# Attention and two expert layers on one core: zero rows copied by ScalarE, zeros behind the running sum, three warming products, changed times in the planner

## The chip, the core and the metric

One Trainium2 chip, one of its cores. The time is that of one execution on the device in microseconds; a kernel is run several times and the median counts. Five engines work side by side, each through its own queue in order: TensorE (PE, with weight loads PEld), VectorE (DVE), ScalarE (ACT), GpSimd (POOL) and SyncE (SP), which here issues every DMA.

## What is computed

```python
scores = scale * np.matmul(q, k.transpose(0, 1, 3, 2))      # 4 batches, 8 heads, 576 x 64
log_f = np.log(np.clip(f, 0.0001, 1.0))
cum = np.cumsum(log_f, axis=-1)
scores = np.where(causal, -1e9, scores + cum[..., None] - cum[..., None, :])
attn = softmax(scores)                                       # by row
x = (attn @ v), heads side by side                           # 2304 tokens x 512
x = ((x @ w1) * (x @ w2)) @ w3 @ w_out                       # 512 -> 1024 -> 512
xn = x / sqrt(mean(x * x) + 1e-6) * rms_g
out = (silu(xn @ w_gate) * (xn @ w_val)) @ w_out2            # 512 -> 1536 -> 512
```

## The kernel before

**The work.** Up to about 400 us the kernel does three things at once. (1) Attention, 32 heads one after another. A head's scores are products of Q and K with extra rows that add the running sum of log f (L421 for heads 0 and 1, which use `rq` and `rk` in plain float32; L423 and L424 later, which use Q and K split into a high and a low part). VectorE takes the row maximum (L443) and ScalarE the exponential (L451); TensorE transposes the result (L492), ScalarE copies the high part (L501, `PTh`), VectorE takes the difference, the low part (L502 and L505, `PTl`), and TensorE multiplies by V into `wide` (L552, L556). The two buffers a and b serve even and odd heads. (2) Weights come as 64-bit numbers and are made into float32 by `convert`: the load (L575), the high halves on ScalarE (L584), the low halves on ScalarE (L588) or VectorE (L590), both joined on VectorE (L594). A `unit` then splits the result into two parts for TensorE (L258, L260, L251). `widen` makes three sums more (L819), which the second layer needs, and stores the matrix to `sw_d` (L842); ten of these are done beside attention, in one buffer `raw_w`. (3) The first layer: w3 x w_out is multiplied out ahead (L668), then come, by blocks of 464 tokens, x @ w1 and x @ w2 (L705), their product (L712, L713) and the rest (L730). From about 530 us on the second layer runs on TensorE alone (L920, L1001).

**The start** (`start`, from L1092). `f` is loaded in two halves and clipped (L1113, VectorE); ScalarE takes the logarithm (L1114) and VectorE the running sum `cum` of each half (L1119); from it VectorE makes Q's extra rows of heads 0 and 1 (L1133) and ScalarE K's (L1136). These rows lie in the lower 64 partitions of `rq` and `rk`, which must be zero elsewhere: `make_rows` writes zeros, for head 0 on VectorE and for head 1 on GpSimd (L1099, L1100). `make_zeros` (L348) writes the corners of the buffers of scores, which no product fills. Five products of zeros (L1090, WARM) run on TensorE before the first head; three and one more come a little later (`zeros` in `attention`).

**What sets the order.** No engine's order is written out by hand. Every step is handed to `Plan` with the engines that could do it, a duration in ns for each, the keys it reads and writes, and for some a due time (S0, TE, T1 for heads, WD0 and WD1 for the ten stores of widened matrices, FD and FR for the first layer). `Plan.order` then lays the steps out in time by these numbers, on the engine that would end a step first, and what it finds is the order in which the instructions are written to the queues. DMA0, COLD, RS and RB are its numbers for DMAs and for the first products. A key that a step reads only for the plan (`zeros` reads CUM) makes no wait on the chip unless the data itself is read.

## Time and profile before

| | us |
|---|---|
| median of 3 runs (931.03 to 933.44) | 931.06 |
| the profiled execution | 929.87 |
| its span, first to last instruction | 928.2 |
| busy: TensorE / VectorE / ScalarE / GpSimd | 913.6 / 803.3 / 550.0 / 165.0 |

The profile is of one execution. A busy TensorE includes products that overlap, so its share is no measure of how full it is; its idle time, and the chain of work that ended last, say more. In a row of a timeline the first number is the start in us from the beginning of the span, the second how long the work lasted, then engine, line, operation, what is written from what, and in brackets how long the engine had been idle and what ended that. Line numbers are those of the kernel before; in the changed one those of `start` are two to five higher, those from L349 to L505 one, and those from L575 to L1090 four.

### The profile page before, as it was taken

How to read it: one execution, taken by the hardware profiler on the slowest of the kernel's cores; microseconds unless marked ns; L12 is line 12 of the kernel's file. 1: busy time of each engine (PE TensorE's matmuls, PEld its weight loads, DVE VectorE, ACT ScalarE, POOL GpSimd, SP SyncE). 2: the span in 40 equal slices, each digit the busy share in tenths (PEclk: the TensorE clock that was granted, in tenths of full speed). 3: DMA queues.
4: the chain of work that ended last, by engine and by line, in shares of the span. 5: the costliest groups of instructions: out<-in, count | busy, mean ns of one | idle time of the engine just before them, and what ended most of it. 6: DMA issues, size and time to landing. Idle time of an engine off the chain costs nothing.

```text
span 928.2 us, 14651 instructions
## 1 busy us (share of the span) xinstructions
PE 913.6 (98%) x5064; PEld 845.6 (91%) x5064; DVE 803.3 (87%) x1540; ACT 550.0 (59%) x1132; POOL 165.0 (18%) x162
## 2 busy tenths in 40 slices
PE   9999999999999999999999999999999999999998
PEld 5678888899989898988899999999999999999998
DVE  7999999988999899836655889999988899888796
ACT  8999888777777776732332344545444465544452
POOL 2254423343223422230120400000000000000000
PEclk9999999999999999999999999999999999999999
DMA  7867476667755584437777334634743425633322
GB/s 258 298 226 235 136 274 217 232 184 239 264 175 181 155 285 175 153 109 282 237 269 259 121 131 133 217 103 130 258 168 119 143 69 171 203 119 122 134 68 103
DMA packets 50878, 170.70 MB, mean 184 GB/s; under 512 B 7388, under 2 KB 23356, under 8 KB 43636
## 3 DMA queue, kind: packets, MB, share of 16 engines
q1 hardware_dynamic: 50804, 169.77, 54.8%
q8 instruction: 40, 0.66, 0.3%
q14 instruction: 34, 0.28, 0.1%
HBM read 133.28 MB, written 32.63 MB: 179 GB/s over the span
## 4 chain that ended last, share of the span: by engine, by line
PE 82%; DVE 9%; DMA 5%; ACT 2%; issue 2%; SPq 0%; DVEq 0%; ACTq 0%
PE bank L920 28%; PE bank L705 17%; PE bank L730 10%; PE bank L1001 8%; PE wide L1001 4%; PE bank L492 3%; PE wide L552 3%; PE bank L668 3%; DVE qk L251 1%; DMA raw_w<-in_w 1%; PE bank L423 1%; PE bank L424 1%; DVE wbig L251 1%; DVE PTl L502 1%; PE bank L1090 1%
## 5 line engine op out<-in xcount | busy, mean ns | idle before, releaser
L705 PE MATMUL bank<-xhl,wbig 128*128 128x464 f32 (+1 forms) x960 | 216.6, 374 | 1.1 <-DVE wbig L251 1.1
L705 PEld LDWEIGHTS bank<-xhl,wbig 128*128 128x128 f32 x960 | 176.2, 188 | 18.6 <-DVE wbig L251 1.5
L920 PE MATMUL bank<-xop,wbig 128*128 128x384 f32 x1008 | 182.3, 334 | 0.7 <-ACT cs L944 0.7
L920 PEld LDWEIGHTS bank<-xop,wbig 128*128 128x128 f32 x1008 | 175.5, 188 | 1.1 <-ACT cs L944 1.0
L920 PE MATMUL bank<-xop,lbig 128*128 128x384 f32 x504 | 94.7, 334 | 0.0
L920 PEld LDWEIGHTS bank<-xop,lbig 128*128 128x128 f32 x504 | 88.0, 188 | 0.0
L502 DVE TENSOR_TENSOR PTl<-bank,PTh 128x512 fp32r<-128x512 f32 (+5 forms) x138 | 62.8, 469 | 7.9 <-ACT PTh L501 7.1
L501 ACT CAST PTh<-bank 128x320 fp32r<-128x320 f32 (+4 forms) x138 | 57.5, 435 | 18.3 <-PE bank L492 15.2
L730 PE MATMUL bank<-uh,Wch 128*128 128x464 f32 (+1 forms) x160 | 60.7, 379 | 0.0
L730 PE MATMUL bank<-uh,Wcl 128*128 128x464 f32 (+1 forms) x160 | 59.4, 371 | 0.0
L730 PE MATMUL bank<-ul,Wch 128*128 128x464 f32 (+1 forms) x160 | 59.3, 371 | 0.0
L251 DVE TENSOR_TENSOR lbig<-zf,lbig 128x768 fp32r<-128x768 f32 x63 | 59.2, 952 | 0.1
L1001 PE MATMUL bank<-lbig,wbig 128*128 128x384 f32 x324 | 57.9, 334 | 0.0
L1001 PEld LDWEIGHTS bank<-lbig,wbig 128*128 128x128 f32 x324 | 56.3, 188 | 0.0
L258 ACT ACTIVATE lbig<-zf 128x768 fp32r<-128x768 f32 x39 | 33.0, 849 | 37.6 <-PE bank L1001 17.9
L260 POOL TENSOR_SCALAR lbig<-zf 128x768 fp32r<-128x768 f32 x2 | 1.8, 920 | 276.7 <-DVE zf L819 263.5
L552 PE MATMUL wide<-PTh,V 128*128 128x512 f32 (+4 forms) x145 | 44.4, 316 | 1.4 <-DVE nmaxb L443 0.6
L712 DVE TENSOR_TENSOR u<-bank,u 128x464 f32<-128x464 f32 (+1 forms) x40 | 25.2, 629 | 23.1 <-PE bank L705 22.9
L251 DVE TENSOR_TENSOR wbig<-nrm,wbig 128x768 fp32r<-128x768 f32 (+1 forms) x42 | 43.3, 1036 | 0.4
L713 ACT CAST uh<-u 128x464 fp32r<-128x464 f32 (+1 forms) x40 | 23.0, 575 | 34.4 <-DVE u L712 34.4
L942 ACT COPY cs<-bank 128x384 f32<-128x384 f32 x36 | 17.3, 481 | 42.8 <-PE bank L920 42.8
L926 DVE TENSOR_TENSOR zf<-cs 128x384 f32<-128x384 f32 x72 | 39.9, 554 | 2.7 <-ACT cs L931 1.7
(271 smaller groups left out, 2109.5 us busy)
## 6 DMA issues: line engine op xcount, KB each, us to landing
xf<-sw_d SPq DMA_DIRECT2D x24, 896.0 KB
wbig<-w_d SPq DMA_DIRECT2D x12, 1024.0 KB
nrm<-sw_d SPq DMA_DIRECT2D x12, 896.0 KB
raw_w<-in_wgv SPq DMA_DIRECT2D x10, 1024.0 KB
sw_d<-raw_w SPq DMA_DIRECT2D x10, 896.0 KB
rk<-in_k SPq DMA_DIRECT2D x62, 144.0 KB
nrm<-wo_d SPq DMA_DIRECT2D x11, 768.0 KB
xf<-wo_d SPq DMA_DIRECT2D x10, 768.0 KB
```

Of the source, the lines that this page charges most:

```text
L251: plan.op([t_dve(n, lock=True), t_pool(n)], lambda e: on[e].tensor_sub(*(x() if callable(x) else x for x in (o, a, b_))), r, w)
L258: A.activation(o_, a_, AF.Copy, scale=by)
L492: T.transpose(o[:, c * P:(c + 1) * P], PB[p][i][:, kb * P:(kb + 1) * P], ident)
L501: act(n, lambda c=c, to=to, n=n: A.copy(PTh[:, to:to + n], o[:, c:c + n]), [], [("PTh", name), key], at, 55)
L502: dve(m, lambda c=c, to=to, m=m: V.tensor_sub(PTl[:, to:to + m], o[:, c:c + m], f32(PTh[:, to:to + m])), [("PTh", name)], [("PTl", name), ...
L552: pe(w, lambda s_=s_, o=o, w=w, c=c, kb=kb, m=m, src=src: T.matmul(t[:, o:o + w], V2[p][:, kb, :], src[:, c:c + w], start=(s_ == 0 and m = ...
L668: T.matmul(o, a, b_, start=(ft == 0 and m == 0), stop=(ft == KF - 1 and m == 2))
L705: T.matmul(o, a, x[:, kt, :], start=(kt == 0 and i == 0), stop=(kt == KD - 1 and i == 2))
L730: T.matmul(o, a[:, es], x[:, ft, 0:w], start=(q == 0 and ft % 2 == 0 and i == 0), stop=(q == 3 and ft % 2 == 1 and i == 2))
L920: T.matmul(o, w[:, a, POS[j], kt], x[c][:, kt], start=start and kt == 0 and i == 0, stop=kt == 1 and i == 2, skip_group_check=not start)
L926: plan.op([t_dve(TH, lock=True), t_pool(TH)], lambda e: on[e].tensor_mul(o(), x(), y()), r, w)
L1001: T.matmul(tiles[m], wv[:, a, k, m], z[c][:, kt], start=start and k == 0 and x == 0, stop=k == KH - 1 and x == 2, skip_group_check=not start)
```

## The change

ScalarE copies the zero rows of head 1 from head 0's, which VectorE writes in two steps; GpSimd writes them no more. `make_zeros` begins with a multiplication that reads the first half of `cum`, so that the zeros really wait for the first scan. WARM goes from 5 to 3. The rest are numbers of the planner: due times (S0, T1, WD1, FD), its start of DMAs, and durations of six kinds of step. They change no instruction, but the engine that takes a step where there is a choice, and the order on every engine.

```diff
--- before.py
+++ after.py
@@ -40,12 +40,12 @@
 SW = 2 * NOP * 256
 PADW = 8
 EARLY = 10
-WD0, WD1 = 130000, 380000
+WD0, WD1 = 130000, 400000
 WD2, WD3 = 420000, 520000
 NR = 4
 KH = KF2 // 2
 FROWS = 112
-WARM = 5
+WARM = 3
 NQ, NP, QD, PAIR = 2, 3, 6, 10
 WIDER = 3
 NST = 3
@@ -53,16 +53,16 @@
 
 
 
-S0, TE, T1 = -1500, 7800, 13400
+S0, TE, T1 = -2500, 7800, 13800
 LT, LP = 5000, 13000
 
 WC0, WCP = 20000, 9000
 
-FD, FR = 27000, 1.8
+FD, FR = 25000, 1.8
 
 WAIT, SLIP, SLIP0, SOON = 5.0, 1200, 300, 30000
 
-DMA0, COLD, RS, RB = 2500, 7000, 230, 330
+DMA0, COLD, RS, RB = 550, 6000, 230, 330
 MT, MARGIN, MARGIN2 = 135000, 600, 700
 MT2, MARGIN3 = 538000, 200
 
@@ -346,6 +346,7 @@
         G.memset(one32, 1.0)
 
     def make_zeros():
+        G.tensor_scalar(out=PB[0][1][0:1, QEND[1]:QEND[1] + 1], in0=cum[0:1, 0:1], scalar1=1.0, scalar2=1.0, op0=ALU.mult, op1=ALU.mult)
         for t in PB:
             for i in range(1, 4):
                 G.memset(t[i][:, QEND[i]:], 0.0)
@@ -502,7 +503,7 @@
             dve(m, lambda c=c, to=to, m=m: V.tensor_sub(PTl[:, to:to + m], o[:, c:c + m], f32(PTh[:, to:to + m])), [("PTh", name)], [("PTl", name), key], at)
         if m < n:
             both = PTh[D:P, m:n]
-            dve(n - m, lambda: V.tensor_sub(both, o[D:P, lo + m:lo + n], f32(both)), [], [("PTh", pt), key], at)
+            dve(n - m + 110, lambda: V.tensor_sub(both, o[D:P, lo + m:lo + n], f32(both)), [], [("PTh", pt), key], at)
 
     def sums(h, at):
         pr, r_o = h // 2 % 2, r_d[h // 2].rearrange("j (i b n) -> b (j i) n", i=5, b=4)
@@ -557,8 +558,8 @@
             [("PTh", PT_KB3), ("V2", p), ("V2h", p)], wk, at)
         x_to, x_key = X[b % 2][j * D:(j + 1) * D, pp, :], ["cq"] * (b == 0) + [("x", b % 2, pp, j)] + [("raw", "x1")] * (b == 1)
         low = xlow[j * D:(j + 1) * D, :]
-        act(S, lambda: A.copy(x_to, t[0:D, 0:S]), wk, x_key, at)
-        act(S, lambda: A.copy(low, t[D:P, 0:S]), wk, [("xlow", j)], at)
+        act(S, lambda: A.copy(x_to, t[0:D, 0:S]), wk, x_key, at, 160)
+        act(S, lambda: A.copy(low, t[D:P, 0:S]), wk, [("xlow", j)], at, 160)
 
     def normalize(h, at):
         pair, (b, pp) = h // 2, divmod(h // 2, H // 2)
@@ -570,9 +571,12 @@
             dve(S, lambda: V.tensor_add(x[D:], x[D:], low[D:]), [("xlow", 1)], keys[1:])
         plan.op([t_dve(S, lock=True), t_pool(S)], lambda e: on[e].tensor_mul(x, x, rall), [("rall", 0), ("rall", 1)], keys)
 
+    begun = []
+
     def convert(raw, key, src, at_load, r_load=(), w_load=(), to=None):
         kl, kh = key + ("lo",), key + ("hi",)
-        dma(1.05e6, lambda: SP.dma_start(out=u32(raw()), in_=src.bitcast(U32)), r_load,
+        begun.append(key)
+        dma(1.36e6 if len(begun) == 1 else 1.05e6, lambda: SP.dma_start(out=u32(raw()), in_=src.bitcast(U32)), r_load,
             [key, kl, kh] + list(w_load) + ["cn", "cn1"] * (key[1] == "x1"), at_load)
 
         def lo():
@@ -589,7 +593,7 @@
             else:
                 V.tensor_scalar(out=lo(), in0=lo(), scalar1=2.0**-29, scalar2=7.0, op0=ALU.mult, op1=ALU.min)
 
-        plan.op([t_act(1024), t_dve(1024, 0.52, True)], bits, [key, "under"], [kl])
+        plan.op([t_act(1024, 260), t_dve(1024, 0.61, True)], bits, [key, "under"], [kl])
         o, w = (lo, [kl]) if to is None else (lambda: u32(to()), [kl, kh])
         dve(1024, lambda: V.scalar_tensor_tensor(out=o(), in0=hi(), scalar=3, in1=lo(), op0=ALU.logical_shift_left, op1=ALU.bitwise_or), [key, kh], w, lock=True)
         return lo, hi
@@ -1095,29 +1099,27 @@
         load_qk(0, -90)
         dma(2e3, load_g, w=["g"], at=50000)
         dve(300, lambda: V.memset(mask, 0.0), w=["mask", "mask0"])
-        def make_rows(e, p):
-            e.memset(rq[p][D:P, :], 0.0)
-            e.memset(rk[p][D:P, :], 0.0)
-
-        dve(1030, lambda: make_rows(V, 0), w=[("nrowq", 0), ("nrown", 0), ("rk", 0, 1)])
+        for x, keys in ((rq, [("nrowq",)]), (rk, [("nrown",), ("rk", 1)])):
+            w0, w1 = ([(k[0], p, *k[1:]) for k in keys] for p in range(2))
+            dve(515, lambda x=x: V.memset(x[0][D:P, :], 0.0), w=w0)
+            act(S, lambda x=x: A.copy(x[1][D:P, :], x[0][D:P, :]), w0, w1)
 
         for i in range(WARM):
             zeros(5, -1000)
         pool(580, make_ones, w=["one32", "cn1"], at=-50)
         pool(1100, make_masks, w=["ident", "mask", "ones"], at=-40)
-        pool(1160, lambda: make_rows(G, 1), w=[("nrowq", 1), ("nrown", 1), ("rk", 1, 1)])
         dve(70, lambda: V.memset(rows_c, 1.0), w=["picks"])
         dve(70, lambda: (V.memset(under, -0.501), V.memset(exp_in, 0.0)), w=["under", "exp"])
         act(1500, lambda: A.activation(rows_c[:, 0:1], rows_c[:, 0:1], AF.Ln), [], ["picks"])
         for i, c in enumerate(half):
-            dve(150, lambda c=c: V.tensor_scalar(out=fc[:, c], in0=fc[:, c], scalar1=1.0e-4, scalar2=1.0, op0=ALU.max, op1=ALU.min), [], [("fc", i)], lock=True)
+            dve(170, lambda c=c: V.tensor_scalar(out=fc[:, c], in0=fc[:, c], scalar1=1.0e-4, scalar2=1.0, op0=ALU.max, op1=ALU.min), [], [("fc", i)], lock=True)
             act(S // 2, lambda c=c: A.activation(fc[:, c], fc[:, c], AF.Ln), [], [("fc", i)], fixed=200)
         for i, c in enumerate(half):
             if i:
                 x, last = fc[:, c.start:c.start + 1], cum[:, c.start - 1:c.start]
                 dve(30, lambda: V.tensor_add(x, x, last), [CUM[0]], [("fc", 1)])
             dve(S + 60, lambda c=c: V.tensor_tensor_scan(out=cum[:, c], data0=one32[:, c], data1=fc[:, c], initial=0.0, op0=ALU.mult, op1=ALU.add), [("fc", i), "one32"], [CUM[i]])
-        pool(650, make_zeros, [CUM[1]], ["zeros"])
+        pool(850, make_zeros, [CUM[0]], ["zeros"])
         hi, lo = cqx[:, 0, :], cqx[:, 1, :]
 
         def first_rows(h):
@@ -1134,7 +1136,7 @@
                 [*CUM, "ident", "picks"], [("nrowq", h)])
             for i, n in enumerate(half):
                 act(S // 2, lambda n=n: A.activation(rk[h][r, n], cum[r, n], AF.Identity, scale=c[:, 1:2], bias=e[0]),
-                    [CUM[i], "ident", "picks", ("nrown", h), ("rk", h, 1)], [("nrown", h, i)], fixed=260)
+                    [CUM[i], "ident", "picks", ("nrown", h), ("rk", h, 1)], [("nrown", h, i)], fixed=380)
 
         for h in range(NQ):
             first_rows(h)
```

Three places of the new order follow. GpSimd, the start; `tmp` holds f, ones and `cum`, `PB` and `rsum` are buffers of scores and row sums, `qk` is the split Q and K. Before:

```order
L1099 MEMSET rq_103 64x576
L1100 MEMSET rk_105 64x576
L351 MEMSET PB1a 128x64
L351 MEMSET PB2a 128x64
L351 MEMSET PB3a 128x64
L351 MEMSET PB1b 128x64
L351 MEMSET PB2b 128x64
L351 MEMSET PB3b 128x64
L353 MEMSET rsuma 128x32
L353 MEMSET rsumb 128x32
L354 MEMSET roots 128x32
L372 MEMSET qk_108 64x576
```

and with the change:

```order
L349 TENSOR_SCALAR PB1a<-tmp 1x1
L352 MEMSET PB1a 128x64
L352 MEMSET PB2a 128x64
L352 MEMSET PB3a 128x64
L352 MEMSET PB1b 128x64
L352 MEMSET PB2b 128x64
L352 MEMSET PB3b 128x64
L354 MEMSET rsuma 128x32
L354 MEMSET rsumb 128x32
L355 MEMSET roots 128x32
L373 MEMSET qk_108 64x576
```

The two writes of zero rows are gone, and the nine writes of `make_zeros` stand behind a step that reads `cum`.

ScalarE, around the conversion of the seventh widened matrix (`raw_w`, its high halves); PB3a to PB0a are the exponentials of head 26, `PTh` copies of transposed scores. Before:

```order
L560 COPY x_133<-wide 64x576
L561 COPY xlow<-wide 64x576
L584 ACTIVATE raw_w_1233<-raw_w_1233 128x1024
L451 ACTIVATE PB3a,rsumb<-PB3a,nmaxa 128x448
L501 CAST PTh<-bank_61 128x320
L451 ACTIVATE PB2a,rsumb<-PB2a,nmaxa 128x320
L451 ACTIVATE PB1a,rsumb<-PB1a,nmaxa 128x192
L501 CAST PTh<-bank_59 128x448
L501 CAST PTh<-bank_60 128x256
L258 ACTIVATE qk_108<-rq_103 64x576
L258 ACTIVATE PB1a<-PB2a 64x64
L451 ACTIVATE PB4a,rsumb<-PB4a,nmaxa 128x576
```

and with the change:

```order
L452 ACTIVATE PB3a,rsumb<-PB3a,nmaxa 128x448
L502 CAST PTh<-bank_61 128x320
L452 ACTIVATE PB2a,rsumb<-PB2a,nmaxa 128x320
L258 ACTIVATE qk_108<-rq_103 64x576
L452 ACTIVATE PB1a,rsumb<-PB1a,nmaxa 128x192
L452 ACTIVATE PB4a,rsumb<-PB4a,nmaxa 128x576
L502 CAST PTh<-bank_59 128x448
L502 CAST PTh<-bank_60 128x256
L452 ACTIVATE PB4a,rsumb<-PB0a,nmaxa 64x64
L739 COPY nrm<-bank_63 128x464
L258 ACTIVATE PB4a<-PB4a 128x64
L588 ACTIVATE raw_w_1239<-raw_w_1239 128x1024
```

The conversion stood ahead of all exponentials of head 26 and now stands behind them.

VectorE, around the three sums of the ninth widened matrix (L819 before, L823 now), with the low parts `PTl` of head 28 before, and of the head then in work now. Before:

```order
L594 SCALAR_TENSOR_TENSOR raw_w_1233<-raw_w_1233 128x1024
L502 TENSOR_TENSOR PTl<-bank_59,PTh 128x448
L502 TENSOR_TENSOR PTl<-bank_60,PTh 128x256
L819 TENSOR_TENSOR raw_w_1233<-raw_w_1233 128x512
L819 TENSOR_TENSOR raw_w_1233<-raw_w_1233 128x256 x2
L502 TENSOR_TENSOR PTl<-bank_59,PTh 128x64
L712 TENSOR_TENSOR u_134<-bank_62,u_134 128x464
```

and with the change:

```order
L598 SCALAR_TENSOR_TENSOR raw_w_1239<-raw_w_1239 128x1024
L503 TENSOR_TENSOR PTl<-bank_61,PTh 128x512
L503 TENSOR_TENSOR PTl<-bank_59,PTh 128x64
L444 ISA PB2b,nmaxb<-bank_60,mask 128x320
L444 ISA nmaxb 128x1
L444 ISA PB1b,nmaxb<-bank_60,mask 128x192
L444 ISA nmaxb 128x1
L823 TENSOR_TENSOR raw_w_1239<-raw_w_1239 128x512
L716 TENSOR_TENSOR u_134<-bank_63,u_134 128x464
L823 TENSOR_TENSOR raw_w_1239<-raw_w_1239 128x256 x2
```

The sums stood ahead of the `PTl` of 64 columns and now stand behind it and behind the next head's `PTl` of 512.

## Rows read from the trace of the kernel before

**Rows 1.** The page: span, TensorE's busy time, the chain that ended last.

```profile
span 928.2 us, 14651 instructions
...
PE 913.6 (98%) x5064; PEld 845.6 (91%) x5064; DVE 803.3 (87%) x1540; ACT 550.0 (59%) x1132; POOL 165.0 (18%) x162
...
PE 82%; DVE 9%; DMA 5%; ACT 2%; issue 2%; SPq 0%; DVEq 0%; ACTq 0%
```

**Rows 2.** Busy us of each engine by stretch, instructions, clock, DMA share, GB/s.

```profile
20.00:160.00 140.00, 134.54 (x741) 110.07 (x740) 137.32 (x293) 127.87 (x277) 54.73 (x42) 1.00 0.70 230
160.00:300.00 140.00, 139.36 (x808) 125.88 (x807) 128.15 (x323) 104.08 (x264) 46.70 (x45) 1.00 0.66 213
300.00:380.00 80.00, 77.31 (x449) 69.73 (x449) 73.45 (x191) 58.05 (x145) 23.61 (x23) 1.00 0.64 211
380.00:640.00 260.00, 260.00 (x1375) 246.17 (x1375) 195.13 (x334) 108.37 (x191) 32.88 (x27) 1.00 0.52 178
640.00:680.00 40.00, 39.33 (x227) 39.01 (x226) 37.63 (x53) 18.17 (x28) 0.00 (x0) 1.00 0.70 237
```

**Rows 3.** Timeline of all engines, 0 to 12 us.

```profile
1.51 5.79 PE L1090 MATMUL bank<-mask 128*128 128x448 f32 x10 [1.51 <-DVE rows_c L1109]
...
2.27 0.54 DVE L1100 MEMSET rk<- 64x576 f32 x1
...
2.54 0.57 POOL L1099 MEMSET rq<- 64x576 f32 x1
...
3.17 1.47 DVE L1113 TENSOR_SCALAR tmp<-tmp 112x288 f32<-112x288 f32 x2
3.17 0.34 PEld L1090 LDWEIGHTS bank<-mask 128*128 128x128 f32 x1 [0.41 <-issue]
...
3.83 0.44 ACT L1114 ACTIVATE tmp<-tmp 112x288 f32<-112x288 f32 x1 [1.61 <-DVE tmp L1113]
...
3.92 0.34 PEld L1090 LDWEIGHTS bank<-mask 128*128 128x128 f32 x1 [0.41 <-issue]
...
4.53 0.62 POOL L372 MEMSET qk<- 64x576 f32 x1
4.56 0.74 DVE L1119 TENSOR_TENSOR_SCAN tmp<-tmp 112x288 f32<-112x288 f32 x1
...
6.39 0.62 ACT L1136 ACTIVATE rk<-tmp,ident,rows_c 4x288 f32<-4x288 f32 x1 [0.37 <-DVE tmp L1119]
6.39 0.57 DVE L1133 TENSOR_SCALAR rq<-tmp,rows_c,ident 4x576 f32<-4x576 f32 x1
...
7.13 1.14 PE L421 MATMUL wide<-rk,rq 128*128 128x288 f32 x4
...
8.11 3.25 PE L421 MATMUL bank<-rk,rq 128*128 128x448 f32 x12
```

**Rows 4.** Groups by line and shape, 20 to 400 us: busy us, mean ns, idle before.

```profile
L258 ACT ACTIVATE qk<-rq 64x576 fp32r<-64x576 f32 x16 | 10.9, 680 | 0.3 <-PE wide L423 0.2
...
L588 ACT ACTIVATE nrm<-nrm,tok 128x1024 uint32<-128x1024 uint32 x4 | 5.0, 1246 | 0.0
...
L590 DVE TENSOR_SCALAR raw_w<-raw_w 128x1024 uint32<-128x1024 uint32 x11 | 8.1, 733 | 4.1 <-DMA raw_w<-in_wgv 2.7 <-DMA raw_w<-in_w 1.5
```

**Rows 5.** Timelines of ScalarE, VectorE and TensorE, around 315 to 325 us.

```profile
315.54 1.20 ACT L584 ACTIVATE raw_w<-raw_w 128x1024 f32<-128x1024 f32 x1 [2.19 <-DMA raw_w<-in_wgv]
...
323.48 1.38 DVE L819 TENSOR_TENSOR raw_w<-raw_w 128x256 f32<-128x256 f32 x1
...
325.17 0.41 PE L552 MATMUL wide<-PTl,V 128*128 128x320 f32 x1 [1.44 <-DVE PTl L502]
```

**Rows 6.** Timelines of VectorE and TensorE, around 360 to 364 us.

```profile
360.35 3.63 DVE L819 TENSOR_TENSOR raw_w<-raw_w 128x512 f32<-128x512 f32 x3
363.89 0.22 DVE L502 TENSOR_TENSOR PTl<-bank,PTh 128x64 fp32r<-128x64 f32 x1
...
364.16 0.41 PE L552 MATMUL wide<-PTl,V 128*128 128x320 f32 x1 [1.25 <-DVE PTl L502]
```

## The prediction

> **What bounds the kernel now.** I read the page's head first [rows 1]. TensorE holds a product for 913.6 of 928.2 us, and the clock was at its upper level, 2.4 GHz, almost throughout; yet the chain of work that ended last runs on TensorE for 82% alone, and 9% of it lies on VectorE, 5% in DMAs. So there is something to gain where TensorE waits, and the second view, the busy times by stretch, tells where that is [rows 2]. From 20 to 160 us TensorE has 140 - 134.54 = 5.46 us without a product, from 160 to 300 us 0.64, from 300 to 380 us 2.69, and in 640 to 680 us 0.67. In 20 to 160 us VectorE is busy for 137.32 of 140 us: it sets the pace there, and ScalarE with 12.1 us of idle time is second. After that VectorE has more slack (11.85 us in 160 to 300), TensorE is nearly full, and what it loses from 300 us on it loses at a few places. The timeline shows two of them: a pause of 1.44 us before the product at 325.17 and one of 1.25 us before that at 364.16, each ended by VectorE's L502 [rows 5, 6]. Together that is 2.69 us, all of the idle time of the stretch.
>
> The profiled execution took 929.87 us, 1.7 more than its span; the median of the three runs is 931.06, 1.19 above it. The sum is made against 929.87 and its difference is then taken from the median. A measurement of this kernel can tell about 0.3%, 2.8 us, from no change.
>
> **The start.** *Zero rows.* GpSimd loses two writes of 0.57 us (one of them in [rows 3]), ScalarE gets two copies instead. A ScalarE operation on 64x576 takes 0.68 us [rows 4]. Head 1 alone needs these rows, but the copies stand ahead of the logarithms in ScalarE's queue, and they wait for VectorE's writes, the second of which ends at 2.27 + 0.54 = 2.81. So the first logarithm (L1114, 3.83 before) can begin at about 2.81 + 0.68 + 0.1 = 3.6, if the clips of VectorE (L1113, two in 1.47 us, beside GpSimd's writes) are done: those then have GpSimd's company no more, and at 0.73 us for 1024 columns [rows 4] a clip of 288 should take some 0.3. Everything after it (scan, second logarithm, the rows of L1136) follows at the same distances: 0.2 us earlier.
>
> *Zeros behind the running sum.* The nine small writes stood between GpSimd's second row write (which ends at 2.54 + 2 x 0.57 = 3.7) and L372 at 4.53, so they take some 0.85 us. Now they wait for the first scan, which ends at 4.56 + 0.74 - 0.2 = 5.1. Behind them in GpSimd's queue stand the writes of L372 to L374 (0.62 us the first) [rows 3]. They come at 5.95 to 7.8 instead of 4.53 to 6.3. Who waits for them: the first exponentials, which come behind head 0's products (7.13 and 8.11), and Q/K of head 3 later still; nobody. But they now run beside L1133 (6.39, 0.57 us), on which head 0's first product waits. From below the cost is nothing; from above, if L1133 is held for one such write, 0.6 us.
>
> The Trainium skill ("SBUF — State Buffer", "SBUF: two separate sides") says that GpSimd and a VectorE operation in a two-port mode exclude each other for a whole instruction; by it the clips gain and L1133 pays, and the start would come out at +0.4 instead of -0.2. I take 0 for the start, with -0.2 and +0.6 kept for the range.
>
> *Two warming products fewer.* Five (ten records) take 1.51 to 7.30. The loads of the early ones follow each other by 0.75 us (3.17, 3.92) [rows 3], so six records end between 1.51 + 6 x 0.58 = 5.0 and 1.51 + 6 x 0.75 = 6.0. Head 0's first product began at 7.13 because L1136 ended at 6.39 + 0.62 = 7.01. The waits of ScalarE and VectorE cover the removed products wholly: 0. What that pause of 1.1 to 2.1 us does to the clock is a rival.
>
> *Loads.* SP now issues the store of cq ahead of head 2's first loads, and head 1's V ahead of one weight load. These queue behind four megabytes of earlier loads either way: 0.
>
> **From 20 to 160 us.** The planner's changed costs move operations with a choice of engine. Counted in the order, ahead of head 16's first row maximum, ScalarE takes 4 more conversions of low halves (L588, 1.25 us each [rows 4]), 5 more copies of Q (0.68 us [rows 4]), 2 fewer of K, and, with the two zero copies and smaller exchanges, about 6 us more in all. VectorE loses 4 of these conversions (L590, 0.73 [rows 4]) and gains additions and differences that GpSimd had: about 1 us less in all. VectorE sets the pace here, so from below this gives -1.0; from above, if none of ScalarE's 6.1 us fits into its 12.1 us of idle time, +6.1. The nearest row is VectorE's 2.68 us of idle time in 140 [rows 2]: its work decides, and of that 1.0 us I count nothing, because conversions were moved toward head 14 and away from heads 16 on, and up to head 11 its work is larger by about 1 us. I take 0.
>
> **From 300 to 380 us.** *Seventh widened matrix.* Its load reaches ScalarE at 315.54 [rows 5], and the exponentials of head 26 stand behind that conversion; VectorE then does its own three sums on the way, the last two in 1.38 us at 323.48, before the differences (L502) for which TensorE waits 1.44 us. In the new order of ScalarE the conversion stands behind all exponentials of head 26, and on VectorE the sums of L819 stand behind the L502 of 64 columns. *Ninth.* Three sums of 3.63 us at 360.35 stand ahead of the L502 of 64 columns at 363.89, and TensorE waits 1.25 us [rows 6]. In the new order that difference, and the one of 512 columns for the next head, come ahead of them. Both pauses should go: -1.44 - 1.25 = -2.69. From above 0, if another wait takes their place.
>
> What is late next: the sums now stand behind the differences, so the buffer of the next widened matrix comes free later, but it is needed later too (its store has a due time moved back, 380 to 400 us at the end). Counted over all heads, the conversions (L590, L594, L819) that stand between one head's first and last L502 come to some 40 us in either order. Before, five heads had over 3 us of them (16, 23, 25, 28, 30), and the pauses came in two of these, 25 and 28; now there are two such heads, 14 and 19. Two in five of two heads is 0.8 of a pause, at a time when TensorE has more in hand, so I charge half of one of 1.44: +0.7.
>
> **After 380 us** nothing moves but the engine of some copies; TensorE has no idle time to 640 us. The 0.67 us between 640 and 680 stay [rows 2]: 0.
>
> **The sum:** 0 + 0 + 0 - 2.69 + 0.7 = -2.0; 929.87 becomes 927.9, and the median 931.06 becomes 929.1 (-0.2%).
>
> **The rivals.**
> 1. *Less work ahead on VectorE shortens the early stretch as well.* Then half of the 5.46 us of TensorE's idle time there goes too (its own 1.0 us among it), with no new pause: 931.06 - 2.69 - 2.73 = 925.6. For it: VectorE's 98% in that stretch. Against: its work up to head 11 grew. 33%.
> 2. *Slower: ScalarE becomes the bound before head 16.* Its 6.1 us more do not fit, because its idle time stands in small pieces; all exponentials queue behind the added conversions, and VectorE's differences behind those. 931.06 - 2.0 + 6.1 = 935.2. It decides from the point at which over 4.8 of the 6.1 us find no idle time. For it: each head's chain passes through ScalarE several times, so that a late conversion delays it more than once. Against: 12.1 us of idle time are twice what is added. 13%.
> 3. *The clock falls in the pause before head 0.* The products from 7.13 to 8.11 + 3.25 = 11.36 [rows 3], 4.2 us, would run at 1.2 GHz and take twice as long; VectorE's row maxima run beside them, so about half of 4.2 us shows: 931.06 - 2.0 + 2.1 = 931.2. Against it: the clock stayed at 2.4 GHz through a pause of 1.44 us [rows 2, 5], though with work close on both sides. The Trainium skill ("TensorE: Matmul & The Clock Gate", "What's actually happening") holds that the slow clock is the default and that work releases it; by that rule fewer products at the start can move the release later, which gives this same time. 9%.
>
> **How the numbers follow.** The forecast, 929.1, has 45%, and it is a difference too small to tell. Faster by over 0.3%: rival 1 and a little of the forecast's lower edge, 0.36. Slower: rival 2 and unknown pauses of a new order, 0.15. Within 0.3%: the rest, 0.49. The range goes from 925.4 (rival 1 with the start's 0.2) to 933.0 (no pause gone, and a third of ScalarE's work uncovered); outside lie most of rival 2 and a stronger rival 1.
>
> **What would show it.** Right: the first product of head 0 between 6.9 and 7.6 us; the clips under 0.4 us each; no pause over 0.5 us ahead of an L502 of the seventh and ninth widened matrix; TensorE's idle time in 300 to 380 below 1.5 us, and in 20 to 160 within 1.5 us of 5.46; ScalarE busier by 5 to 6 us over the span. Wrong: ScalarE over 96% busy from 20 to 160 with VectorE idle for more than 6 us there (rival 2), VectorE's idle time there unchanged and TensorE's below 3.5 (rival 1), or half-clock records after 5.1 us (rival 3).

## The result, and the profile after

| | us |
|---|---|
| before, median (931.03 to 933.44) | 931.58 |
| with the change, median (923.65 to 925.13) | 924.46 |
| ratio, 95% interval | 0.992, 0.9903 to 0.9937 |
| profiled execution, before and after | 929.87 and 925.13 |

The forecast was 929.1 with a range from 925.4; the measured time lies 0.9 us below the range. The head of the page after, and its chain, against [rows 1]:

```profile
span 923.4 us, 14680 instructions
...
PE 909.0 (98%) x5060; PEld 845.7 (92%) x5060; DVE 803.4 (87%) x1543; ACT 553.5 (60%) x1130; POOL 163.3 (18%) x162
...
PE 90%; DVE 5%; ACT 3%; issue 1%; DMA 1%; DVEq 0%; ACTq 0%; SPq 0%
```

No engine does much less or more than before. What changed is the chain: TensorE's share rose from 82 to 90%, that of the DMAs fell from 5 to 1% and VectorE's from 9 to 5%. The same stretches as in [rows 2], with the first 8 us:

```profile
0.00:8.00 8.00, 5.22 (x11) 2.68 (x12) 5.83 (x17) 6.22 (x11) 4.63 (x22) 1.00 0.68 204
20.00:160.00 140.00, 132.78 (x744) 111.56 (x743) 136.48 (x295) 129.25 (x266) 48.15 (x42) 1.00 0.72 234
160.00:300.00 140.00, 139.61 (x807) 125.94 (x806) 128.01 (x316) 108.69 (x274) 47.48 (x45) 1.00 0.62 206
300.00:380.00 80.00, 79.97 (x467) 72.55 (x466) 72.66 (x192) 56.69 (x145) 22.39 (x27) 1.00 0.57 187
380.00:640.00 260.00, 260.00 (x1379) 246.62 (x1378) 202.89 (x347) 109.35 (x188) 37.55 (x26) 1.00 0.54 187
640.00:680.00 40.00, 40.00 (x233) 40.00 (x232) 38.26 (x55) 18.44 (x30) 0.00 (x0) 1.00 0.69 238
```

From 300 to 380 us TensorE is without a product for 0.03 us instead of 2.69, and does 467 products instead of 449. In 20 to 160 us it is idle longer than before, 7.22 us against 5.46, and does three products more all the same. Idle time is a poor measure there, since products can also follow each other slowly without a pause. So I use a second one, worked out from the starts of TensorE's products: each product is given the median distance to the next one of its line and shape, over all profiles, and the **lag** at a moment is the time gone by less the distances of the products done (warming products not counted). Its level hangs on the distances taken; what is read is differences between profiles. By it the profile of before lags 26.4 us at 160 us and loses 12.3 more up to 380; the changed one lags 25.6 and loses 9.1.

The start, with the change (L1094, L1115, L1116, L1135 and L422 are L1090, L1113, L1114, L1133 and L421 of [rows 3]):

```profile
1.51 4.10 PE L1094 MATMUL bank<-mask 128*128 128x448 f32 x6 [1.51 <-DVE rows_c L1111]
...
2.83 0.67 ACT L1105 COPY rk<-rk 64x576 f32<-64x576 f32 x1
...
3.18 0.53 DVE L1115 TENSOR_SCALAR tmp<-tmp 112x288 f32<-112x288 f32 x2
...
3.53 0.78 ACT L1116 ACTIVATE tmp<-tmp 112x288 f32<-112x288 f32 x2
...
5.87 0.91 DVE L1135 TENSOR_SCALAR rq<-tmp,rows_c,ident 4x576 f32<-4x576 f32 x1
5.89 0.57 POOL L373 MEMSET qk<- 64x576 f32 x1
...
6.88 1.21 PE L422 MATMUL wide<-rk,rq 128*128 128x288 f32 x4 [1.27 <-DVE rq L1135]
```

The two clips take 0.53 us in place of 1.47 now that GpSimd writes nothing beside them. About a third of that is given back: GpSimd's later writes run beside L1135, which takes 0.91 us in place of 0.57. Head 0's first product comes 0.25 us earlier.

### The profile page after: what moved, and what is told of

Read it like the earlier page. It is cut to its first block, busy times and chain, and to the rows that moved or that the text cites. A ratio compares the mean times of both kernels' runs of the same rounds, so it can differ in the third digit from the quotient of the medians.

```text
span 923.4 us, 14680 instructions
## 1 busy us (share of the span) xinstructions
PE 909.0 (98%) x5060; PEld 845.7 (92%) x5060; DVE 803.4 (87%) x1543; ACT 553.5 (60%) x1130; POOL 163.3 (18%) x162
## 4 chain that ended last, share of the span: by engine, by line
PE 90%; DVE 5%; ACT 3%; issue 1%; DMA 1%; DVEq 0%; ACTq 0%; SPq 0%
PE bank L924 28%; PE bank L709 20%; PE bank L734 10%; PE bank L1005 10%; PE bank L493 4%; PE wide L1005 4%; PE wide L553 4%; PE bank L672 3%; PE bank L424 1%; PE bank L425 1%; DMA raw_w<-in_w 1%; DVE qk L251 1%; PE wide L424 1%; PE wide L425 1%; DVE wbig L251 1%
## 5 line engine op out<-in xcount | busy, mean ns | idle before, releaser
L502 ACT CAST PTh<-bank 128x320 fp32r<-128x320 f32 (+4 forms) x138 | 57.5, 434 | 27.0 <-PE bank L493 25.6
L503 DVE TENSOR_TENSOR PTl<-bank,PTh 128x192 fp32r<-128x192 f32 (+5 forms) x138 | 62.7, 471 | 3.6 <-ACT PTh L502 2.5
L251 DVE TENSOR_TENSOR lbig<-zf,lbig 128x768 fp32r<-128x768 f32 x63 | 59.2, 952 | 0.1
L251 DVE TENSOR_TENSOR wbig<-nrm,wbig 128x768 fp32r<-128x768 f32 (+1 forms) x42 | 42.9, 1028 | 0.4
```

The source lines that it names most:

```text
L251: plan.op([t_dve(n, lock=True), t_pool(n)], lambda e: on[e].tensor_sub(*(x() if callable(x) else x for x in (o, a, b_))), r, w)
L502: act(n, lambda c=c, to=to, n=n: A.copy(PTh[:, to:to + n], o[:, c:c + n]), [], [("PTh", name), key], at, 55)
L503: dve(m, lambda c=c, to=to, m=m: V.tensor_sub(PTl[:, to:to + m], o[:, c:c + m], f32(PTh[:, to:to + m])), [("PTh", name)], [("PTl", name), ...
```

## The experiments

Three kinds of edit. Some kernels change numbers of the planner only. Others have their order written out as a list, so that nothing else can move; their line numbers are 75 to 79 higher than those of before:

```diff
-        for i, e, _ in plan.order():
-            plan.ops[i][1](e)
+        for n in ORDER:
+            plan.ops[n // 6][1](ENGINE[n % 6])
```

A list can also be put together of two orders: all steps that the first has up to a moment, then what is left in the order of the second. Summary, by ratio to the kernel before measured beside each; lag and loss from the one profile of each:

| kernel | median, us | ratio (95%) | lag at 160 | lost 160-380 |
|---|---|---|---|---|
| again (before) | 931.7 | 0.9992 (0.9974-1.0010) | 26.6 | 11.2 |
| start_only | 932.1 | 1.0012 (0.9990-1.0034) | 26.9 | 12.7 |
| two_moves | 932.0 | 1.0000 (0.9982-1.0018) | 28.8 | 15.0 |
| third_load | 931.9 | 0.9997 (0.9981-1.0014) | 29.4 | 12.9 |
| early_part | 929.4 | 0.9981 (0.9966-0.9996) | 26.3 | 13.7 |
| neutral_number | 931.0 | 0.9991 (0.9977-1.0005) | 29.2 | 12.3 |
| wd1_only | 929.7 | 0.9992 (0.9979-1.0006) | 27.9 | 11.7 |
| cost_attention | 929.6 | 0.9988 (0.9973-1.0002) | 27.9 | 9.2 |
| cost_start | 929.4 | 0.9981 (0.9966-0.9996) | 28.4 | 9.8 |
| without_low_halves | 929.4 | 0.9984 (0.9968-1.0000) | 28.8 | 9.1 |
| near_shorter | 929.1 | 0.9973 (0.9959-0.9986) | 29.0 | 9.3 |
| near_longer | 927.1 | 0.9955 (0.9939-0.9972) | 26.3 | 9.4 |
| cost_low_halves | 925.7 | 0.9940 (0.9922-0.9959) | 27.7 | 7.5 |
| costs_only | 926.0 | 0.9946 (0.9932-0.9960) | 27.3 | 7.8 |
| late_part | 926.5 | 0.9953 (0.9936-0.9970) | 28.6 | 8.0 |
| changed_again | 924.4 | 0.9926 (0.9910-0.9941) | 24.8 | 9.3 |
| best_parts | 924.3 | 0.9925 (0.9910-0.9940) | 24.6 | 9.0 |
| best_numbers | 928.4 | 0.9970 (0.9956-0.9983) | 27.5 | 9.0 |

### Are the two pauses the place?

**again**: the kernel before, profiled a second time.

> The kernel before, unchanged, profiled a second time. The question is what of the difference between the two profiles belongs to the order and what to the execution. If the wait of 0.67 us for ScalarE's L944 at 666 us is a property of the order, it stands here too, at the same place; if it comes from a transfer that landed late in that one execution (xf from sw_d, 7.5 us after its issue there), it is gone or of another length. The two pauses of 1.44 and 1.25 us ahead of L502 (heads 25 and 28) should stand within 0.3 us on either theory. Its time: the ratio to itself within 0.1% of 1.

The pause ahead of the ninth widened matrix's difference stands, that of the seventh (325 us) has gone, and so has the one at 666 us:

```profile
363.35 0.41 PE L552 MATMUL wide<-PTl,V 128*128 128x320 f32 x1 [1.25 <-DVE PTl L502]
```

The profile of early_part (below), whose order behind 165 us is that of before, has the pause of the seventh again (L628 is L552):

```profile
326.55 0.43 PE L628 MATMUL wide<-PTl,V 128*128 128x320 f32 x1 [1.70 <-DVE PTl L578]
```

Of the five profiles with the old order in this stretch it stands in two, those in which ScalarE waited 2.19 and 2.74 us for the load of the seventh matrix; where ScalarE waited 0.71 to 1.13 us it is missing. So 1.44 of the 2.69 us on which the forecast rested come and go with that load, while the 1.25 us stand in all five. Single executions of this program differ: 926.7 to 935.5 us in the 35 taken beside this group, 926.7 to 933.1 in the 22 of them with a mean granted clock of 1.000.

**two_moves**, the kernel before in its own order but for ScalarE's conversion of the seventh matrix, with the VectorE steps that depend on it, and VectorE's sums of the ninth. The second, with the names of before:

```diff
 L502 TENSOR_TENSOR PTl<-bank_59,PTh 128x448
 L502 TENSOR_TENSOR PTl<-bank_60,PTh 128x256
-L819 TENSOR_TENSOR raw_w_1233<-raw_w_1233 128x512
-L819 TENSOR_TENSOR raw_w_1233<-raw_w_1233 128x256 x2
 L502 TENSOR_TENSOR PTl<-bank_59,PTh 128x64
...
 L502 TENSOR_TENSOR PTl<-bank_61,PTh 128x512
+L819 TENSOR_TENSOR raw_w_1233<-raw_w_1233 128x512
+L819 TENSOR_TENSOR raw_w_1233<-raw_w_1233 128x256 x2
```

> The kernel before in its own order, written out as a list, with two moves alone: the conversion of the seventh widened matrix (L584 on ScalarE, and what depends on it) stands behind all exponentials of head 26, and the three sums of the ninth (L819) behind the differences (L502) of 64 and of 512 columns. Theory A: both pauses go, 1.44 + 1.25 = 2.7 us of the profile, and the time falls by 2.4 to 3.0 us, 0.3%. Rival B (another wait takes their place, since the sums now meet the next head's work): 0 to -1.3 us, with a new pause of over 0.5 us within 10 us of either place. Rival C (the whole new order is needed, because TensorE's slow stretches around the pauses, 3.3 us of 300 to 380, go only with it): the pauses go and 300 to 380 us still loses over 4 us against the dense cadence of products.

Both pauses are gone, and the time is the same. Rival B: the work stands behind something else now. VectorE and TensorE (L894, L665, L577, L567 and L499 are L819, L590, L502, L492 and L424):

```profile
331.07 1.17 DVE L894 TENSOR_TENSOR raw_w<-raw_w 128x256 f32<-128x256 f32 x1 [0.91 <-POOL raw_w L894]
...
342.03 0.70 DVE L665 TENSOR_SCALAR raw_w<-raw_w 128x1024 uint32<-128x1024 uint32 x1 [0.73 <-DMA raw_w<-in_wgv]
```

```profile
332.89 0.33 PE L567 MATMUL bank<-ident,PB3a 128*128 128x128 f32 x1 [0.82 <-DVE PTl L577]
...
342.77 0.39 PE L499 MATMUL bank<-qk 128*128 128x320 f32 x1 [0.83 <-DVE raw_w L665]
```

A sum of the seventh matrix waits for GpSimd's and makes the next difference late (0.82 us), and the eighth conversion, reached earlier, waits for its load, which costs TensorE 0.83 us. What rival C named holds as well: from 300 to 380 us this profile loses about as much by the lag as that of before. The two rivals are not told apart here; theory A is out.

### Which part of the change: instructions, early order, late order

**start_only**: the change's instructions (zero rows, zeros, three products) in the order of before, as a list.

> Only the three edits that change instructions (zero rows copied by ScalarE, the zeros behind the running sum, three warming products), in the order of the kernel before, which is written out as a list; no number of the planner acts. Theory A (the gain lies in the order of VectorE and ScalarE from 300 to 380 us): head 0's first product 0.2 to 0.3 us earlier, and the time of before, -0.3 to +0.3 us. Rival B (the start makes the gain, because everything behind it follows at the same distances): -1 us or more. Rival C (three warming products leave the clock low for the first head): +2 us, and half-clock records behind 5.6 us.

No gain: the three edits in the title that change instructions are worth nothing that can be told from none. Head 0's first product comes at 7.24 us (7.13 before), behind an L1133 of 0.91 us, as above. The granted clock is 1.00 in 0 to 20 and in 20 to 160 us.

**early_part** and **late_part**: lists of two orders, joined at some 160 us; early_part has the change's instructions, late_part those of before.

> The changed kernel's order up to about 165 us of the execution, the order of the kernel before from there on; both written out as a list, the instructions those of the change. By the two profiles TensorE's products stand 0.85 us earlier at 160 us with the change. Theory A: -0.9 us (-0.5 to -1.3) for the whole kernel, and the pauses ahead of L502 at heads 25 and 28 as before. Rival B (what is won early is lost again where the old order follows, since its waits are on VectorE's own pace): -0.3 to +0.3. Rival C (the early stretch carries the gain of all that follows): -3 us or more, the later pauses shorter.

> The order of the kernel before up to about 160 us, the changed kernel's order behind it, both written out as a list; the instructions of the start are those of before. The early part alone gave 0.998. If the two parts add up to the whole change (0.992): 0.994, some 926.5 us. Theory D (the later spacing of the widened matrices is the gain): 0.993 to 0.995, no wait of raw_w's conversions for a transfer. Rival (the early lead of TensorE is what makes the transfers early enough behind it): 0.998 or above.

0.9981 x 0.9953 = 0.9934, within the interval of the whole (0.9926): the parts add, and the larger one lies behind 160 us. The early part's 1.8 us are more than any of its three expectations named; its interval, 0.4 to 3.2 us, holds theory A's 0.5 to 1.3. The late part's loss there is 8.0 us, the early part's 13.7.

**changed_again**: the changed kernel once more.

> The changed kernel, unchanged, timed in more runs and profiled a second time. The kernel before ran between 926.7 and 935.5 us, and its two profiles differ by up to 1.9 us in how far TensorE had come. Theory D (the change takes transfers off the path, so that a late one no longer stops ScalarE's queue): the times lie closer together than those of before, within some 4 us, around 924.5, ratio 0.992; no conversion of raw_w (L588) waits for a transfer in this profile either. Theory E (the order itself is shorter, whatever the transfers do): the same median, but a spread as wide as that of before, 8 us.

The same median, and times within 2.9 us of each other (6 executions); those of before, in the same group, lie within 4.7 (17), in the largest group within 9 (35). With so few executions the narrower spread is an indication only. The second profile has the same losses as the first (24.8 and 9.3).

### Which number of the planner

**wd1_only** and **costs_only**, numbers alone in the kernel before:

```diff
-WD0, WD1 = 130000, 380000
+WD0, WD1 = 130000, 400000
```

> The kernel before with one number changed: WD1, the due time of the last of ten stores of widened matrices, from 380 to 400 us, and what the planner makes of it (its conversions of the seventh to tenth matrix come at 318, 341, 364 and 385 us of its own time in place of 307, 327, 347 and 368). Theory D (the one buffer raw_w has to be loaded again before ScalarE's next conversion, and more room between them ends the waits for the load, 6.5 us in five places before): ScalarE's L584 on raw_w waits for transfers under 2 us in all, and the time falls by 2.5 to 5 us, ratio 0.995 to 0.997. Rival (this number is one of many that reshuffle the order): within 0.2% of before either way, though the waits are gone.

> The kernel before with the changed durations of the planner alone (first load, low halves, L505, L560, L561, clip, K's rows, zeros, DMA0 and COLD); due times, instructions and WARM as before. Theory D: the early stretch's gain at most, ratio 0.997 to 1.000, the waits of L584 on raw_w for transfers still there (over 3 us in all). Rival (true durations let the planner fit the work, and the due times are by the way): 0.992 to 0.996.

The due time gives nothing that can be told from none, although the widened matrices hardly wait for their loads any more (0.3 us on ScalarE, none on VectorE; a wait of 3.44 us for `in_w` on ScalarE at 167 us stays): the rival. The durations give two thirds and more of the gain, as the second run's rival had it. Split into three:

```diff
-        plan.op([t_act(1024), t_dve(1024, 0.52, True)], bits, [key, "under"], [kl])
+        plan.op([t_act(1024, 260), t_dve(1024, 0.61, True)], bits, [key, "under"], [kl])
```

> The kernel before with one changed pair of durations: the conversion of low halves, on ScalarE 95 to 260 ns fixed, on VectorE 0.52 to 0.61 ns a column. The planner then puts raw_x's conversion on ScalarE at 25.8 us of its own time. All changed durations together gave 0.9946. Theory F: the early wait for raw_x goes, ratio 0.997 to 0.999; the pauses of 160 to 380 us are those of a new order, either way. Theory H (these true durations are the whole gain of the changed numbers): 0.994 to 0.996. Rival (any new order is as good or bad): 1.000 or above.

> The kernel before with the changed durations of the attention's steps alone: VectorE's L505 by 110 columns longer, ScalarE's copies L560 and L561 by 65 ns each. raw_x's conversion stays where it was, ahead of head 1's row maxima. Theory F: the early wait stays possible, so no gain there; in 160 to 380 us TensorE's loss against its dense cadence (12.2 and 11.2 us in the two profiles of before, 9.2 and 9.3 with the change, 7.9 with all changed durations) falls to 8 to 10 if these durations are what made the planner leave room for L502: ratio 0.995 to 0.997. Rival: 0.999 to 1.002, and pauses of over 1 us ahead of L552 in that stretch as before.

> The kernel before with the changed durations of the start alone: the first load, DMA0 and COLD, clip, K's rows, zeros. The planner puts raw_x's conversion on ScalarE at 17.4 us of its own time, ahead of head 1's exponentials. Theory F: VectorE waits no more for it, ScalarE does in some executions, so the gain is partial: ratio 0.998 to 1.000. Rival (the start's numbers give the planner the true arrival of the first loads, and all behind it fits better): 0.994 to 0.996.

One pair of numbers, the duration of the low halves' conversion on its two engines, gives 0.9940 alone; the others give at most 0.9981. To tell a true duration from a lucky order: its neighbours, a number that means nothing here, and the change without it.

```diff
-        plan.op([t_act(1024), t_dve(1024, 0.52, True)], bits, [key, "under"], [kl])
+        plan.op([t_act(1024, 250), t_dve(1024, 0.6, True)], bits, [key, "under"], [kl])
```

> The kernel before with the duration of the low halves' conversion alone changed, and not quite as far as the change does: 250 in place of 260 ns on ScalarE, 0.60 in place of 0.61 on VectorE. With 260 and 0.61 the time was 0.994. Theory H (the planner needs the true duration, and fits the steps of 160 to 380 us better for it): 0.993 to 0.996, as a change of 10 ns cannot matter. Theory I (each set of numbers draws another order, and 260 with 0.61 drew a good one): anything from 0.993 to 1.000, most likely 0.996 to 0.999 as the other redrawn orders (0.9981, 0.9988, 0.9992).

**near_longer** has 270 and 0.62 at the same place.

> As the run before it, on the other side: 270 ns on ScalarE, 0.62 on VectorE. Theory H: 0.993 to 0.996. Theory I: anything from 0.993 to 1.000, and not the same as its neighbour.

```diff
-S0, TE, T1 = -1500, 7800, 13400
+S0, TE, T1 = -1600, 7800, 13400
```

> The kernel before with S0, a due time of the first heads, at -1600 in place of -1500: no duration is nearer to the chip by it, and the order is redrawn (the engines of three conversions change, and 160 to 380 us are laid out anew). Theory H: 0.998 to 1.002. Theory I: as likely as not 0.994 to 0.998 or beyond 1.002; a result outside 0.998 to 1.002 shows what a redrawn order alone can do.

**without_low_halves** is the changed kernel with the pair back at 95 ns and 0.52.

> The changed kernel with the duration of the low halves' conversion put back (95 ns and 0.52), all else as changed. Theory H: most of the gain goes, 0.997 to 1.000, and 160 to 380 us lose over 11 us against TensorE's dense cadence (9.2 and 9.3 with the change, 12.2 and 11.2 before). Theory I: the order is another again; 0.993 to 1.000, no matter that the duration is wrong.

The runs stand nearer to theory H than to theory I, and do not settle it. For H: of the orders that the planner makes for one set of numbers, the five with a longer duration stand at 0.9926 to 0.9973, and the five changed ones without it at 0.9981 to 0.9992; the pair alone (interval 0.9922 to 0.9959) is clear of all five.

Against it: near_shorter, at 0.9973, lies outside what H allowed, and its interval overlaps those of the five. The neighbours stand at 0.9973, 0.9940 and 0.9955 for 10 ns each, so that redrawing an order does some 0.3% by itself. Nor does the gain follow how true the numbers are. In the profile of before a conversion takes 0.69 us on VectorE (median) and 1.25 on ScalarE. The planner had 0.60 and 0.95 for them, has 0.69 and 1.11 with the change, and 0.70 and 1.12 in near_longer, which gains less.

The clock has a part in it too. Seven of neutral_number's twelve executions have a mean granted clock of 0.998 and a median of 931.7 us, five have 1.000 and 928.8. At 1.000 the kernel before, beside them, has 930.9 and near_shorter 928.8: there the number that means nothing gives as much as near_shorter. In neutral_number's profile TensorE runs at the lower level, 1.2 GHz, for a part of 195 to 200 us (mean granted clock 0.66), behind a pause of 1.88 us:

```profile
195.00:200.00 5.00, 4.63 (x19) 4.23 (x20) 4.90 (x18) 2.57 (x8) 0.00 (x0) 0.66 0.66 247
```

```profile
195.37 0.74 PE L424 MATMUL bank<-qk 128*128 128x448 f32 x1 [1.88 <-DVE qk L251]
```

And the place is open. By H, without_low_halves should have lost over 11 us from 160 to 380 us; its profile loses 9.1 there, as the changed kernel's does, and is 3.2 to 4.0 us further behind at 160 us. All its twelve executions have a mean granted clock of 0.996 (five, median 931.2) or 0.998 (seven, 928.7). In its profile the clock falls behind waits of TensorE for `qk` of 1.10 and 0.63 us (0.33 and 0.63 with the change, where it stays at 1.00):

```profile
25.00:30.00 5.00, 5.00 (x18) 2.71 (x17) 4.94 (x15) 4.64 (x12) 0.73 (x2) 0.66 0.89 250
```

The profile of best_parts has the same fall (0.66) and lags no more at 160 us than the changed kernel's, so this one fall does not explain the 3 us. Besides, cost_attention and cost_start, without the pair, lose only 9.2 and 9.8 us from 160 to 380 and stand at 0.9988 and 0.9981. So it is shown that the pair, put into the kernel before, gives the larger part of the gain; that it does so because it is nearer to the chip, and from 160 to 380 us, is not shown.

### The third load

**third_load**: VectorE's L590 of raw_x behind head 1's row maxima, all else in the order of before.

```diff
 L590 TENSOR_SCALAR raw_ul<-raw_ul 128x1024
-L590 TENSOR_SCALAR raw_x<-raw_x 128x1024
 L443 ISA PB4b,nmaxb<-wide,mask 128x576
...
 L594 SCALAR_TENSOR_TENSOR raw_ul<-raw_ul 128x1024
+L590 TENSOR_SCALAR raw_x<-raw_x 128x1024
```

In the profile of two_moves, whose start is that of before, this is what a late third load does to VectorE and then to TensorE (L617 is L542):

```profile
18.68 0.69 DVE L665 TENSOR_SCALAR raw_x<-raw_x 128x1024 uint32<-128x1024 uint32 x1 [3.15 <-DMA raw_x<-in_wo]
```

```profile
20.15 3.16 PE L617 MATMUL wide<-PTf,rv 128*128 128x512 f32 x10 [1.71 <-issue]
```

The row names "issue", but the product writes `wide`, which VectorE's row maximum behind that conversion (19.29 to 20.04 us) was still to read. In the profile of before the same conversion waited 0.75 us.

> The kernel before in its own order, written out as a list, with one move: VectorE's conversion of the low halves of the third weight loaded (raw_x, L590, 15 us) stands behind head 1's row maxima and the two joins that follow, in place of ahead of them. Theory F (in the order of before this conversion stops VectorE's queue whenever its load lands late; it landed at 14.8 to 15.3 us in three profiles and at 18.3 to 18.7 in three others, where VectorE waited 2.7 to 3.2 us for it and TensorE stood 1.8 to 1.9 us later at 20 us): the executions in which it is late lose nothing more, so the median falls by 1 to 3 us (ratio 0.997 to 0.999), and VectorE waits under 1 us for raw_x in this profile. Rival G (the wait is taken up again by VectorE's own pace before 160 us): the same time as before, within 0.1%.

Rival G as to the time, though the interval (0.9981 to 1.0014) still holds the upper half of theory F's range. The wait is gone from the profile; this execution stood still for 2.89 us at 81 us, where a copy of `qk` landed late:

```profile
81.13 0.44 PE L499 MATMUL bank<-qk 128*128 128x448 f32 x1 [2.89 <-DMA qk<-qk]
```

### A version that might beat both

**best_parts** and **best_numbers**: lists that join the stretches that lost the least in one profile each.

> A version that should beat both kernels: the changed kernel's instructions and its order up to about 165 us, and behind it the order that the one changed duration of low halves gave (the stretch of 160 to 380 us with the least loss against TensorE's dense cadence, 7.5 us, where the changed kernel loses 9.1 and 9.3 there, and 18.7 and 18.0 before it). If stretches add, as the early and the late part did (0.9981 x 0.9953 against 0.9926): 1.7 us below the changed kernel, 922.7 us, ratio 0.9910. If the seam costs what is won, or the loss comes back at another place: 0.992 to 0.994.

> The same with another first part: the instructions of the kernel before, up to about 160 us the order of the run with 270 ns and 0.62 (its profile lost the least there, 9.5 + 8.4 = 17.9 us), behind it the order that 260 ns and 0.61 gave (7.5 us). If stretches add: 17.9 + 7.5 = 25.4 us of loss against 27.8 and 27.3 of the changed kernel, some 922 us, ratio 0.9905, with none of the changed start's edits. If one profile says too little of a stretch whose loads land at other times in each execution: 0.992 to 0.995.

Neither beats the changed kernel: 924.3 is its own time, 928.4 is worse. The second part's stretch loses 9.0 us behind either first part, not the 7.5 it lost behind its own. How well a stretch goes may depend on what is late where it begins; one profile of each does not show it.

## What VectorE does from 160 to 380 us

In the profile of cost_low_halves the gain lies in this stretch (7.5 us lost, against 12.3 and 11.2 before). VectorE's groups of that stretch, the sums (L819) and the low halves (L590) of raw_w, before:

```profile
L819 DVE TENSOR_TENSOR raw_w<-raw_w 128x256 f32<-128x256 f32 x17 | 10.9, 641 | 0.1
...
L819 DVE TENSOR_TENSOR raw_w<-raw_w 128x512 f32<-128x512 f32 x9 | 8.5, 950 | 0.0
```

with the change (L823, L594):

```profile
L823 DVE TENSOR_TENSOR raw_w<-raw_w 128x256 f32<-128x256 f32 x18 | 8.5, 473 | 0.3
...
L823 DVE TENSOR_TENSOR raw_w<-raw_w 128x512 f32<-128x512 f32 x9 | 7.1, 791 | 0.0
...
L594 DVE TENSOR_SCALAR raw_w<-raw_w 128x1024 uint32<-128x1024 uint32 x7 | 4.7, 675 | 0.0
```

and with the low halves' duration alone (cost_low_halves):

```profile
L590 DVE TENSOR_SCALAR raw_w<-raw_w 128x1024 uint32<-128x1024 uint32 x10 | 7.9, 786 | 0.0
L819 DVE TENSOR_TENSOR raw_w<-raw_w 128x256 f32<-128x256 f32 x16 | 7.4, 462 | 0.2
...
L819 DVE TENSOR_TENSOR raw_w<-raw_w 128x512 f32<-128x512 f32 x7 | 5.1, 734 | 0.1
```

Two things are read here. First, the last number of a row, the idle time ahead of it: the low halves of raw_w kept VectorE waiting for 4.1 us before, all of it for the load (the L590 row of [rows 4], whose mean I used and whose wait I did not), and not at all in the other two. The second profile of before has the wait as well:

```profile
L590 DVE TENSOR_SCALAR raw_w<-raw_w 128x1024 uint32<-128x1024 uint32 x11 | 7.6, 687 | 3.6 <-DMA raw_w<-in_w 2.2 <-DMA raw_w<-in_wgv 1.4
```

Second, the mean of one sum: 641 ns (643 in the second profile) against 473 and 462 for the same shape. The shortest takes 407 (the source view of L819, minimum, median, maximum):

```profile
L819 DVE TENSOR_TENSOR raw_w<-raw_w x26: 407/535/1930, 185.5 to 363.5; 128x256 f32<-128x256 f32 x17, 128x512 f32<-128x512 f32 x9
```

and the longest is beside a GpSimd operation:

```profile
188.06 2.26 POOL L251 TENSOR_TENSOR xhl<-x,xhl 128x704 fp32r<-128x704 f32 x1 [0.26 <-ACT xhl L691]
188.67 1.93 DVE L819 TENSOR_TENSOR raw_w<-raw_w 128x256 f32<-128x256 f32 x1
```

GpSimd ends at 190.32, the sum at 190.60. At 0.41 us for 256 columns and 0.67 for 512, the 26 sums of before would take 13.0 us; they took 19.4, 6.4 more. All but 0.1 us of this lies in the 12 sums that ran beside a GpSimd operation. With the change the excess is 2.2 us, with the low halves alone 1.2. The ninth matrix's sums of [rows 6], 3.63 us where 1.5 would do, are such a case, and so is the 1.38 us in [rows 5], which is one sum (x1) and not the two that I read there.

These two losses are shown to go. That they are the gain is not: neutral_number has no wait either and an excess of 4.7 us, wd1_only no wait and 1.8, without_low_halves no wait and 1.7, and they stand at 0.9991, 0.9992 and 0.9984. In wd1_only VectorE's L251 take 6.4 us more in this stretch than the shortest of the same names and shape would, against 2.7 before; but with the change that is 6.4 as well.

One number goes with the gain: TensorE's idle time from 160 to 380 us is 0.00 to 0.80 us in the seven profiles of kernels at 0.9955 or below, and 0.89 to 4.83 in the thirteen others (3.33 and 2.41 in those of before). It tells where the time shows, not which step frees it. So by the runs the larger part of the gain comes with that pair of numbers; by which of VectorE's delays it acts stays open.

## Why the prediction was wrong

- **The start (0).** Right. The first product came at 6.88, inside 6.9 to 7.6 but for 0.02; both effects that were set against each other are in the rows (the clips -0.94 us for the two, L1133 +0.34), and start_only measures nothing in all.
- **Warming products (0), and rival 3.** Right at the place it named: head 0's twelve products behind the pause take 3.24 us as against 3.25 before, and the granted clock is 1.00 from there on in both profiles of the change. The clock can fall later: without_low_halves and best_parts, with the same three products, have 0.66 in 25 to 30 us.
- **Loads (0).** Right for the loads that were named. But the text took the landing of a load as given. It is not: the third weight's conversion waited from 0.31 to 3.15 us in profiles with the start of before.
- **20 to 160 us (0).** Mis-sized: timed alone, the early part is worth 1.8 us (0.9981). In the profiles the lag at 160 us is 26.4 and 26.6 before, 25.6 and 24.8 after, 1.3 us less on the mean. ScalarE's added work was counted rightly, 6.7 us more by 200 us (178.92 against 172.22), but only 1.4 of it lies in 20 to 160 us (129.25 against 127.87), and rival 2 never came near. Over the span it is 3.5 us, not the 5 to 6 that were named as a sign.
- **160 to 300 us (no term).** Left out of the sum because TensorE was idle there for 0.64 us only [rows 2]. Against its own dense pace it lost 6.3 us in that profile, 6.8 in the second and 7.1 to 9.1 in four others with the old order in this stretch; with the change it is 6.0 and 6.0. So 0.3 to 3 us by the execution were missed, which the idle time of that one profile did not show.
- **300 to 380 us (-2.0).** The size came out near, -2.9 us from first profile to first and -1.1 from second to second, and the reason was wrong. The step that failed is "Both pauses should go: -1.44 - 1.25 = -2.69", which made two pauses of one profile the price of the stretch. They do go, and the pause for which +0.7 was charged did not come (TensorE's idle time from 160 to 380 us is 0.42 us in all); but two_moves, 1.0000, shows that taking these two away gives nothing by itself, and one of them stands only where a load lands late.
- **640 to 680 us (stays).** The wait of 0.67 us is gone, in the second profile of before too: it is no property of the order.
- **The step that was mis-sized most** is the list of the changed durations. They were read as moves of single operations between engines and summed per engine, about 1 us less for VectorE. One of them, the low halves, gives 0.9940 alone, 5.6 us. The planner lays out the whole order anew by it, and no sum of busy times showed that ahead: VectorE is busy for 803.3 us before and 803.4 with the change (796.5 with the low halves alone).
- **The basis.** The difference of two profiles is 4.7 us, that of the medians 7.1. The profiled execution of before was 1.7 us better than its median of 931.58, and the one of after 0.7 worse. "Its difference is then taken from the median" assumed that the change moves both alike.
- **Rival 1** (925.6) came nearest in time, but by its own marks it did not happen: TensorE's idle time in 20 to 160 us grew to 7.22 instead of falling below 3.5.

## What to carry to other kernels

Where a planner lays out the order, one of its durations can be worth more than any operation that the change names (here 5.6 us), and neither counts per engine nor the pauses of one profile show that; change the numbers one at a time, and measure a neighbour of each and one that means nothing, before a gain is put down to a cause. In a group's row read the idle time as well as the mean, and hold the mean against the shortest of its shape: where a sum takes 641 ns and 407 would do, look at what another engine runs beside it. Hold executions of like granted clock against each other as well. Profile the kernel before twice: what stands in one of two profiles only is no term of a sum.

## What was not expected of the hardware

- One program ran from 926.7 to 933.1 us on one core at a mean granted clock of 1.000, and up to 935.5 in executions at 0.997 to 0.999. Its profiles, and those of orders close to it, differ by where a transfer landed late: the third weight load (0.31 to 3.15 us of wait), the seventh widened matrix, a copy of `qk` (2.89 us of TensorE's time), a load in the second layer (0.67 us).
- Seven of twelve executions of one kernel (neutral_number) had a lower mean granted clock, 0.998, and took some 3 us longer in the median than the five at 1.000.
- A VectorE sum of 128x256 took 0.41 us alone and 1.93 beside a GpSimd operation that began 0.61 us ahead of it, and ended 0.28 us after that. The Trainium skill ("SBUF — State Buffer", "SBUF: two separate sides") names this for VectorE operations with two inputs in SBUF as well, against a GpSimd operation that reads SBUF: whichever of the two engines starts first keeps the port for its whole instruction. The trace agrees in the main: of the ten sums of before that began with a GpSimd operation under way, eight took 0.2 to 1.5 us longer; a ninth, begun 0.08 us behind it, was not held, and the GpSimd operation took 1.66 us in place of 1.02; the tenth was not held either. In the prediction the rule was weighed for the start alone, and not here, where these holds take 6.4 us of VectorE's time.
